# Sinkhorn routing: one 64-column product for the column sums in place of two, and two reciprocals in place of one

## The chip, the core and the metric

The kernel runs on one core of one Trainium2 chip, as one program. The metric is the device time of one execution in microseconds (us). The five engines have a queue of instructions each and run beside one another: TensorE (PE in the profile, with its weight loads as PEld), VectorE (DVE), ScalarE (ACT), GpSimd (POOL) and SyncE (SP, which here only issues transfers). They wait for one another through semaphores. On-chip data lies in SBUF, results of products in the banks of PSUM; both have 128 partitions.

## The reference

Everything is in 32-bit floats. An attention block with polynomial sketches makes x, of 4352 tokens by 128. A router then balances a matrix P of 4352 tokens by 8 experts with eight Sinkhorn iterations, and eight experts' two-layer networks are summed with P as weights:

```python
logits = x @ w_gate                       # N = 4352, E = 8
P = np.exp(logits - logits.max())
for _ in range(8):
    P /= P.sum(1, keepdims=True) + 1e-09  # each token's row
    P /= P.sum(0, keepdims=True) + 1e-09  # each expert's column
    P *= N / E
for e in range(E):
    out += P[:, e:e+1] * (np.maximum(x @ w1[e], 0.0) @ w2[e])
```

The change is in the column sums and their reciprocals, inside that loop of eight.

## The kernel before, in words

The program has three stages that overlap. The attention stage makes x transposed (tile `xT`, 128 features by 4352 tokens). The unweighted stage runs experts 0 and 1 on part of the tokens while routing isn't finished: `first` (L772) multiplies a 128-feature weight tile with up to 416 tokens into a PSUM bank, ScalarE applies relu into `hb` (L774), VectorE forms differences of these results (L787), and `into` (L836) multiplies results and differences with the second weights and accumulates in four banks `s`. When a group of tokens is complete, ScalarE copies the four banks out (L695 to L712) and VectorE adds the copies (L685, L688). The weighted stage (L1158 and after) does the remaining experts after routing, on x that is already multiplied with P.

TensorE is used in the first two stages as two column halves: a product of 128 rows and 64 columns goes either to the lower half (results in partitions 0 to 63) or to the upper half (64 to 127), and the two halves run beside each other. The order of TensorE's queue is the program's, one queue for both halves. An `into` step for one block holds p1 and p6, then p2 and p4, then p3 and p5, then p7. p1, p2 and p3 read plain results and go to the lower half; p4 to p7 read differences, p4, p5 and p6 go to the upper half, and p7 alternates from block to block. Each step of four L772/L836 products stands some steps behind the one that made its inputs (`LAG = 8` steps).

Routing (`routing`, below) is a generator. P lies in SBUF as 128 partitions by 34 by 8. In one iteration VectorE sums the rows (L602), takes reciprocals (L603), scales (L605) and sums each partition's part of the columns into `cs`, 128 by 8 (L608). Then comes a `yield`: the driver calls `fill`, which puts steps of the unweighted stage into the queues. After it, TensorE adds the 128 partitions by a product with a matrix of ones (L612), which leaves every column sum in every partition of the bank; VectorE takes the reciprocals (L615) and scales P for the next iteration (L618). Since the order of VectorE and TensorE is the program's own (`manual_schedule`), VectorE's queue is: L608, the differences and additions that `fill` put in, L615, L618, L602 and so on. After the eighth iteration VectorE transposes P (L622) and SyncE writes it to DRAM (`pT`, L624), from where the weighted stage loads rows of it, repeated over all partitions (`pb`, L1064). GpSimd multiplies x by them (L1071) and makes sums of weights (L984 to L988).

The banks `a` come from a pool of four, in rotation: the banks of L772 and that of the column sums share it.

Of the kernel before, what the change touches and what calls it, by code (L numbers as in the profile page):

```python
# [11 lines left out]
F32 = mybir.dt.float32  # L12
# [40 lines left out]
def kernel(  # L53
# [12 lines left out]
    nc = tc.nc  # L66
    P = nc.NUM_PARTITIONS
# [3 lines left out]
    E = moe_w_gate.shape[1]  # L71
# [14 lines left out]
    sk = ctx.enter_context(tc.tile_pool(name="sk", bufs=2))  # L86
# [10 lines left out]
    def bank():  # L97
        return aps.tile([P, 512], F32, tag="a", name="a")
# [14 lines left out]
    ones = consts.tile([P, P], F32, name="ones")  # L113
    nc.gpsimd.memset(ones, 1.0)
    warm = [aps.tile([P, 512], F32, tag="a", name="a") for _ in range(2)]
    for _ in range(6):
        for r in range(2):
            for c in range(2):
                rows, cols = slice(64 * r, 64 * (r + 1)), slice(64 * c, 64 * (c + 1))
                nc.tensor.matmul(warm[r][cols, 0:256], ones[rows, cols], ones[rows, 0:1].to_broadcast([64, 256]),  # L120
                                 start=True, stop=True, tile_position=(64 * r, 64 * c))
# [373 lines left out]
    def logits(c):  # L495
        lo, hi = chunks[c]
        pg = bank()[:, 0:hi - lo]
        for b in range(B):
            nc.tensor.matmul(pg[32 * b:32 * (b + 1)], wg, xT[:, b * S + lo:b * S + hi], start=True, stop=True,  # L499
                             tile_position=(0, 32 * b))  # L500
        lgs.append((c, pg))
# [3 lines left out]
    def logits_turned():  # L505
        c, pg = lgs.pop(0)
        lo, hi = chunks[c]
        nc.vector.transpose(out=lgp[:, lo // 32:hi // 32, :].rearrange("p a e -> p (a e)"), in_=pg)
# [69 lines left out]
    def routing():  # L578

        yield 5  # L580
        for c in range(len(chunks)):
            logits(c)
            yield 0.6
            logits_turned()
        lg = lgp[:, :, 0:E]
        mx = sk.tile([P, 1], F32, tag="mx", name="mx")
        nc.vector.tensor_reduce(out=mx, in_=lg, axis=AX.XY, op=Alu.max)
        yield 2.2
        pm = bank()[:, 0:P]
        for s in range(2):  # L590
            nc.tensor.matmul(pm[64 * s:64 * (s + 1)], mx.to_broadcast([P, 64]), ident, start=True, stop=True,
                             tile_position=(0, 64 * s))
        nc.vector.reduce_max(mx, pm, axis=AX.X)
        nc.vector.tensor_scalar(mx, mx, -1.0, 64 * math.log(2.0), op0=Alu.mult, op1=Alu.add)
        pw = p2s[0]
        nc.scalar.activation(out=pw[:, :, 0:E], in_=lg, func=Act.Exp, bias=mx[:, 0:1])

        step = 1.5 * 2.0 ** (23 - 149 + 64)
        nc.vector.tensor_scalar(pw[:, :, 0:E], pw[:, :, 0:E], step, step, op0=Alu.add, op1=Alu.subtract)
        for it in range(ITERS):  # L600
            rs = sk.tile([P, SA], F32, tag="rs", name="rs")
            nc.vector.reduce_sum(rs, pw, axis=AX.X)  # L602
            nc.vector.reciprocal(rs, rs)  # L603
            p1 = p1s[it % 2]
            nc.vector.scalar_tensor_tensor(p1[:, 0:SA], rs.unsqueeze(2).to_broadcast([P, SA, E]), UP,  # L605
                                           pw[:, :, 0:E], op0=Alu.mult, op1=Alu.mult)
            cs = sk.tile([P, E], F32, tag="cs", name="cs")
            nc.vector.reduce_sum(cs, p1.rearrange("p g e -> p e g"), axis=AX.X)  # L608
            yield 4.25
            pc = bank()[:, 0:E]  # L610
            for s in range(2):
                nc.tensor.matmul(pc[64 * s:64 * (s + 1)], ones[:, 0:64], cs, start=True, stop=True,  # L612
                                 tile_position=(0, 64 * s))
            cr = sk.tile([P, E], F32, tag="cr", name="cr")
            nc.vector.reciprocal(cr, pc)  # L615
            last = it == ITERS - 1
            pw = lgp if last else p2s[(it + 1) % 2]
            nc.vector.scalar_tensor_tensor(pw[:, :, 0:E], cr.unsqueeze(1).to_broadcast([P, SA, E]),  # L618
                                           float(N) / E * (1.0 if last else UP), p1[:, 0:SA],
                                           op0=Alu.mult, op1=Alu.mult)  # L620

        nc.vector.transpose(out=lgT.rearrange("p a s -> p (a s)"), in_=lgp.rearrange("p a e -> p (a e)"))  # L622
        for b in (1, 0, 2, 3):
            nc.sync.dma_start(out=pT[:, b * S:(b + 1) * S],  # L624
                                                  in_=lgT[32 * b:32 * b + E].rearrange("p a s -> p (a s)"))
# [977 lines left out]
    with tc.manual_schedule(engines={engines.DVE, engines.PE}):  # L1603
# [38 lines left out]
        for i, n in enumerate(routing()):  # L1642
            if i == 0:
                next(made)
            for _ in range(2 if i > 4 else 0):
                fill(n / 2)
                next(made, None)
            if i < 5:
                fill(n)
# [55 lines left out]
```

## Time and profile before

| what | value |
|---|---|
| three runs | 883.72, 882.86, 883.63 us, median 883.63 |
| the profiled execution | 883.02 us, of which the profile's span is 881.2 |
| TensorE products, weight loads | 875.6 us (99%), 572.4 us (65%) |
| VectorE | 724.0 us (82%), 982 instructions |
| ScalarE, GpSimd | 384.6 us (44%), 262.8 us (30%) |
| granted TensorE clock | full over the whole span |
| column-sum products L612 | 16 products, 32 records, from 123.4 to 170.2 us |
| their reciprocals L615 | 8, from 124.5 to 171.0 us |

How to read it. Busy time is the union of an engine's instructions; the rest of the span it was idle. A row of the timeline gives the start, the time taken, the engine, the line, the operation, output and inputs by the program's names, output and input shapes, how many instructions are merged in the row, and in brackets the idle time ahead of it with what ended it. Each product of this kernel appears as two records of TensorE. [...] A row of the waits has the waiting engine, the tile and line, what it waited for, the total in us, how often, and the longest.

### The profile page before, as it was taken

The numbers are of one execution on the slowest core, as the hardware profiler recorded it, in microseconds if no ns is written. First come the engines' busy times: TensorE is split into PE (matmuls) and PEld (weight loads), VectorE is DVE, ScalarE is ACT, GpSimd is POOL, SyncE is SP. The second block draws the span as 40 slices with busy tenths as digits, with TensorE's granted clock in tenths as the row PEclk, the third lists the DMA queues.
The fourth block names the chain that finished last, engine by engine and source line by source line (L and its number), as shares of the span: only waits on it lengthen the run. The fifth ranks groups of instructions, "written<-read, shape, count | busy, mean of one in ns | idle before, by whom it ended". The sixth has DMA issues, their size and how long they took to land.

```text
span 881.2 us, 26159 instructions
## 1 busy us (share of the span) xinstructions
PE 875.6 (99%) x10828; PEld 572.4 (65%) x10828; DVE 724.0 (82%) x982; ACT 384.6 (44%) x792; POOL 262.8 (30%) x254
## 2 busy tenths in 40 slices
PE   9999999999999999999999999999999999999998
PEld 6788656877788655555555555555555566667876
DVE  8699689978888887778887778888788888888896
ACT  3455557644444433333343333334443344444442
POOL 3131125454433313222222222221323323312431
PEclk9999999999999999999999999999999999999999
DMA  8888399886666554444435544434755557567762
GB/s 260 270 273 264 96 233 245 130 260 195 197 195 198 171 160 128 136 144 128 129 94 144 137 125 126 117 115 109 194 152 148 154 139 216 152 152 220 219 194 49
DMA packets 120887, 149.08 MB, mean 169 GB/s; under 512 B 52288, under 2 KB 79808, under 8 KB 120384
## 3 DMA queue, kind: packets, MB, share of 16 engines
q1 hardware_dynamic: 112656, 136.92, 54.4%
q0 software_dynamic: 6720, 10.19, 5.8%
q8 instruction: 86, 1.41, 0.6%
q10 hardware_dynamic: 1392, 0.28, 0.2%
q14 instruction: 33, 0.27, 0.1%
HBM read 104.86 MB, written 25.99 MB: 148 GB/s over the span
## 4 chain that ended last, share of the span: by engine, by line
PE 99%; DMA 0%; DVE 0%; issue 0%; SPq 0%; DVEq 0%
PE pair L1158 39%; PE s L1311 39%; PE a L772 9%; PE s L836 7%; PE a L336 1%; PE a L465 1%; PE a L306 0%; DMA kx<-in_k_dram 0%; PE s L1323 0%; PE s L375 0%; PE a L429 0%; PE s L395 0%; PE a L499 0%; PE a L375 0%; PE a L395 0%; PE a L612 0%
## 5 line engine op out<-in xcount | busy, mean ns | idle before, releaser
L1158 PE MATMUL pair<-xf,w1x 64*64 64x320 f32 (+3 forms) x4496 | 574.1, 466 | 0.1
L1311 PE MATMUL s<-hb,w 64*64 64x480 f32 (+3 forms) x2544 | 363.4, 466 | 0.0
L1158 PEld LDWEIGHTS pair<-xf,w1x 64*64 64x64 f32 x4496 | 251.9, 133 | 116.7 <-issue 63.5
L1174 DVE CUSTOM_DVE_ANT_0 hb<-pair,copies 128x960 f32<-128x960 f32 (+3 forms) x234 | 214.8, 918 | 101.9 <-PE pair L1158 90.0
L1311 PE MATMUL s<-hb,ws 64*64 64x480 f32 (+3 forms) x1888 | 280.7, 468 | 0.0
L1311 PEld LDWEIGHTS s<-hb,w 64*64 64x64 f32 x2544 | 150.2, 133 | 76.3 <-issue 38.6
L1311 PEld LDWEIGHTS s<-hb,ws 64*64 64x64 f32 x1888 | 113.0, 133 | 56.6 <-issue 29.3
L1071 POOL TENSOR_TENSOR xf<-xT,pb 128x960 f32<-128x960 f32 (+3 forms) x40 | 70.3, 1759 | 241.0 <-ACT turn L1364 184.3
L1079 POOL TENSOR_TENSOR xf<-xf 128x960 f32<-128x960 f32 (+3 forms) x39 | 68.1, 1745 | 222.9 <-ACT turn L1364 141.1
L1171 ACT ACTIVATE hb<-pair 128x640 f32<-128x640 f32 (+3 forms) x86 | 66.4, 773 | 150.2 <-PE pair L1158 148.4
L772 PE MATMUL a<-xT,w 128*64 128x416 f32 (+3 forms) x512 | 123.0, 465 | 0.0
L774 ACT ACTIVATE hb<-a 128x416 f32<-128x416 f32 (+3 forms) x128 | 59.5, 468 | 65.7 <-PE a L772 60.5
L1216 DVE TENSOR_TENSOR hb<-hb 128x960 f32<-128x960 f32 (+3 forms) x78 | 74.8, 959 | 7.9 <-PE pair L1158 0.9
L1364 ACT COPY turn<-s 128x1 f32<-128x1 f32 x134 | 20.9, 156 | 137.5 <-PE s L1311 137.5
L1223 DVE TENSOR_TENSOR hb<-hb 128x960 f32<-128x960 f32 (+3 forms) x78 | 72.8, 933 | 7.4
L1219 DVE TENSOR_TENSOR hb<-hb 128x960 f32<-128x960 f32 (+3 forms) x78 | 75.0, 961 | 2.4 <-ACT hb L1171 0.6
L1252 ACT COPY copies<-pair 128x960 f32<-128x960 f32 (+3 forms) x78 | 59.9, 768 | 35.5 <-PE pair L1158 35.4
L1248 ACT COPY copies<-pair 128x960 f32<-128x960 f32 (+3 forms) x78 | 60.1, 770 | 33.0 <-PE pair L1158 33.0
L1243 ACT COPY copies<-pair 128x960 f32<-128x960 f32 (+3 forms) x78 | 59.9, 768 | 33.0 <-PE pair L1158 28.8
L1220 DVE TENSOR_TENSOR hb<-hb 128x960 f32<-128x960 f32 (+3 forms) x78 | 71.9, 922 | 0.0
L836 PE MATMUL s<-hb,ws 128*64 128x416 f32 (+3 forms) x224 | 71.6, 474 | 0.0
L787 DVE TENSOR_TENSOR hb<-hb 128x416 f32<-128x416 f32 (+7 forms) x84 | 56.8, 679 | 13.5 <-ACT hb L774 10.7
(207 smaller groups left out, 663.2 us busy)
## 6 DMA issues: line engine op xcount, KB each, us to landing
w1x<-w1x SPq DMA_DIRECT2D x87, 256.0 KB, 3.7
w<-w2x SPq DMA_DIRECT2D x71, 256.0 KB, 3.0
ws<-w2x SPq DMA_DIRECT2D x35, 256.0 KB, 3.5
pb<-pT SPq DMA_DIRECT2D x14, 480.0 KB, 4.2
xf<-xf SPq DMA_DIRECT2D x28, 240.0 KB, 3.5
w1x<-w1x SPq DMA_DIRECT2D x7, 896.0 KB, 5.9
ws<-w2x SPq DMA_DIRECT2D x36, 128.0 KB, 3.6
pb<-pT SPq DMA_DIRECT2D x13, 320.0 KB, 3.9
```

The costliest lines, as they stand in the source:

```text
L772: nc.tensor.matmul(ph[sl], loaded_w[j][0][:, P * f + H2 * s:P * f + H2 * (s + 1)], xT[:, at + lo:at + hi], start=True, stop=True, tile_pos ...
L836: nc.tensor.matmul(sums[g][i][H2 * s:H2 * (s + 1)], w, x, start=c == 1, stop=c == per, tile_position=(0, H2 * s))
L1071: nc.gpsimd.tensor_tensor(xf[:, 0:2].rearrange("p b n -> p (b n)"), xT[:, lo:lo + 2 * n], weights.pop(i), op=Alu.mult)
L1079: nc.gpsimd.tensor_tensor(xf[:, 4:6], xf[:, 1:4:2], xf[:, 0:2], op=Alu.subtract)
L1158: nc.tensor.matmul(out[H2 * col:H2 * (col + 1), r], w1[rows, PLACE[form], o:o + H2], xf[rows, x], start=start, stop=stop, tile_position=(H ...
L1171: nc.scalar.activation(out=x, in_=y, func=Act.Relu)
L1174: nc.vector._custom_dve(TENSOR_ADD_SAT, out=flat(out, n), in0=x, in1=flat(y, n), s0=math.inf, s1=0.0)
L1216: nc.vector.tensor_tensor(ts[0], h[3], h[0], op=Alu.subtract)
L1219: nc.vector.tensor_tensor(ts[1], h[3], h[1], op=Alu.subtract)
L1220: nc.vector.tensor_tensor(ts[2], h[1], ts[0], op=Alu.subtract)
L1223: nc.vector.tensor_tensor(ts[3], h[2], ts[2], op=Alu.subtract)
L1311: nc.tensor.matmul(out_[H2 * half:H2 * (half + 1)], w[rows], flat(x, n)[rows, r], start=c == 1, stop=True, tile_position=(H2 * rho, H2 * h ...
```

## The change

The two products of ones with `cs`, one to the upper and one to the lower half, become one, to the lower half. The sums then stand in partitions 0 to 63 of the bank alone. VectorE reads these 64 partitions twice, and writes the reciprocals into the lower and then into the upper 64 partitions of `cr`. The order of everything else on all engines stays. Lines after L612 move up by one in the changed program.

```diff
-            pc = bank()[:, 0:E]
+            pc = bank()[0:64, 0:E]
+            nc.tensor.matmul(pc, ones[:, 0:64], cs, start=True, stop=True, tile_position=(0, 0))
+            cr = sk.tile([P, E], F32, tag="cr", name="cr")
             for s in range(2):
-                nc.tensor.matmul(pc[64 * s:64 * (s + 1)], ones[:, 0:64], cs, start=True, stop=True,
-                                 tile_position=(0, 64 * s))
-            cr = sk.tile([P, E], F32, tag="cr", name="cr")
-            nc.vector.reciprocal(cr, pc)
+                nc.vector.reciprocal(cr[64 * s:64 * (s + 1)], pc)
             last = it == ITERS - 1
             pw = lgp if last else p2s[(it + 1) % 2]
             nc.vector.scalar_tensor_tensor(pw[:, :, 0:E], cr.unsqueeze(1).to_broadcast([P, SA, E]),
```

## The prediction

> **What bounds the kernel now.** I read the page first, top to bottom.
>
> ```profile
> span 881.2 us, 26159 instructions
> PE 875.6 (99%) x10828; PEld 572.4 (65%) x10828; DVE 724.0 (82%) x982; ACT 384.6 (44%) x792; POOL 262.8 (30%) x254
> DVE  8699689978888887778887778888788888888896
> PE 99%; DMA 0%; DVE 0%; issue 0%; SPq 0%; DVEq 0%
> ```
>
> TensorE is busy 99% and the chain that ended last is TensorE for 99%. So a change moves the end only if it shortens TensorE's own stream or makes it wait. The slices say where a wait can arise: VectorE is at 9 in the seventh and eighth slice, 132 to 176 us, which is the routing. So next the window of that stage, and TensorE's waits from 120 to 190 us.
>
> ```profile
> 120.00:175.00 55.00, 55.00 (x353) 38.70 (x351) 50.97 (x96) 36.64 (x77) 27.24 (x28) 1.00 1.02 203
> ```
>
> ```profile
> PEld s L836 <- DVE hb L787: 0.8, 3, 0.3
> PEld pair L1158 <- POOL w1x L988: 0.7, 1, 0.7
> ```
>
> The third pair of numbers in the window is VectorE: 50.97 us of 55, so little idle time is left to swallow more work. TensorE still counts as busy throughout, but its weight loads wait three times for VectorE's differences (L787): in this stage VectorE already sets TensorE's pace at single points. That is where the change acts.
>
> **The change part by part.** One of two products goes, and one reciprocal becomes two, in each of 8 iterations.
>
> ```profile
> L612 PE MATMUL a<-cs,ones x32: 172/188/203, 123.4 to 170.2; 128*64 128x8 f32 x32
> ...
> L615 DVE RECIPROCAL cr<-a x8: 192/200/207, 124.5 to 171.0; 128x8 f32<-128x8 f32 x8
> ```
>
> ```profile
> 170.19 0.23 PE L612 MATMUL a<-cs,ones 128*64 128x8 f32 x2
> 170.28 0.89 PE L772 MATMUL a<-xT,w 128*64 128x416 f32 x3
> ```
>
> *TensorE.* A product is two records (32 for 16 products). What one costs its column half is the distance to the next product's start, 170.28 - 170.19 = 0.09 us, far less than the record's 0.19. The two products stand on different halves, each beside the other half's work. Dropping the second relieves the upper half alone, by at most 8 x 0.09 = 0.72 us; the lower half keeps its product. The relief counts only where the upper half isn't waiting for something later anyway.
>
> [...]
>
> *VectorE.* The second reciprocal has 8 columns too. Halving the partitions saves nothing: below, the 64-partition sum takes 0.59 us like the 128-partition one ahead of it. So the first reciprocal stays at 0.20 us, and the price of the edit is the distance from the first's start to the second's.
>
> ```profile
> 124.47 0.20 DVE L615 RECIPROCAL cr<-a 128x8 f32<-128x8 f32 x1
> 124.70 0.45 DVE L618 SCALAR_TENSOR_TENSOR p<-cr,p 128x272 f32<-128x272 f32 x1
> ...
> 135.68 1.22 DVE L787 TENSOR_TENSOR hb<-hb 128x416 f32<-128x416 f32 x2
> 136.82 0.58 DVE L685 TENSOR_TENSOR z<-z,w 128x416 f32<-128x416 f32 x1
> 137.43 0.59 DVE L685 TENSOR_TENSOR kept<-z,f 128x416 f32<-128x416 f32 x1
> 138.04 0.59 DVE L685 TENSOR_TENSOR kept<-z,m 64x416 f32<-64x416 f32 x1
> ```
>
> Three spacings are on show. An independent instruction on the same partitions starts 0.08 us before its predecessor ends (136.82 against 135.68 + 1.22 = 136.90): price 0.20 - 0.08 = 0.12. The sum into the upper 64 partitions (kept<-z,m) doesn't need the one ahead of it, yet starts 0.02 after its end (138.04 against 137.43 + 0.59): price about 0.215, taking half of the rounded 0.02 and more. A dependent one starts 0.03 after (124.70 against 124.67): price 0.235. The second reciprocal is the middle case, independent and writing from partition 64 after one that wrote from 0. I take 0.215; the ends are 0.12 and 0.235. A price below zero is excluded, since an instruction is added and none gets shorter.
>
> [...]
>
> The added reciprocal waits only for the first. Behind it on VectorE's queue stand the iteration's chain (L618, L602, L603, L605, L608) and then the differences L787, for which TensorE waits at L836. The bank is given back one reciprocal later; no wait row of TensorE names L615.
>
> *What swallows the price, and what passes it on.* VectorE's idle times, and the second to fourth iteration:
>
> ```profile
> 130.84 0.58 DVE L688 TENSOR_TENSOR kept<-x,m 64x416 f32<-64x416 f32 x1 [0.74 <-ACT m L702]
> 131.35 0.19 DVE L615 RECIPROCAL cr<-a 128x8 f32<-128x8 f32 x1
> ...
> 138.66 0.21 DVE L615 RECIPROCAL cr<-a 128x8 f32<-128x8 f32 x1
> ...
> 144.45 0.20 DVE L615 RECIPROCAL cr<-a 128x8 f32<-128x8 f32 x1
> ...
> 150.54 0.59 DVE L688 TENSOR_TENSOR z<-x,z 128x416 f32<-128x416 f32 x1 [0.16 <-ACT x L698]
> ...
> 171.74 1.31 DVE L622 STREAM_TRANSPOSE qT<-kT 128x1088 f32<-128x1088 f32 x1
> ...
> 173.87 1.02 DVE L787 TENSOR_TENSOR hb<-hb 128x832 f32<-128x832 f32 x1 [0.39 <-ACT hb L774]
> ```
>
> TensorE's weight loads at the three waits, and after them the starts of the products:
>
> ```profile
> 143.03 0.13 PEld L836 LDWEIGHTS s<-hb,ws 128*64 128x64 f32 x1 [0.30 <-DVE hb L787]
> ...
> 147.76 0.13 PEld L836 LDWEIGHTS s<-hb,ws 128*64 128x64 f32 x1 [0.18 <-DVE hb L787]
> 147.76 0.13 PEld L836 LDWEIGHTS s<-hb,w 128*64 128x64 f32 x1
> ...
> 167.91 0.13 PEld L836 LDWEIGHTS s<-hb,ws 128*64 128x64 f32 x1 [0.27 <-DVE hb L787]
> ```
>
> ```profile
> 143.03 0.56 PE L836 MATMUL s<-hb,ws 128*64 128x416 f32 x1
> ...
> 148.08 0.51 PE L836 MATMUL s<-hb,w 128*64 128x416 f32 x1
> ...
> 168.05 0.49 PE L836 MATMUL s<-hb,ws 128*64 128x384 f32 x1
> ```
>
> ```profile
> 148.98 0.50 ACT L695 COPY z<-s 64x416 f32<-64x416 f32 x1 [0.21 <-PE s L836]
> ```
>
> Step by step, with price d = 0.215:
> Iteration 1 (124.47) is swallowed: VectorE idles 0.74 us before 130.84 for a ScalarE copy that follows TensorE.
> Iterations 2 to 4 (131.35, 138.66, 144.45) lie in back-to-back work, so the difference awaited at 147.76 comes 3d = 0.645 later. At 143.03 the product took 0.56 where others take 0.51: a late weight load costs 0.05 before the product runs. The second load at 147.76 stands behind the waiting one, on the other half; its product began at 148.08, so it had 148.08 - 147.76 - 0.05 = 0.27 to spare. That product completes the group: ScalarE's copies (148.98) follow it, and VectorE's next start (150.54) follows the copies. From there VectorE is 3d - 0.27 = 0.375 late.
> Iterations 5 to 7 add 3d without idle time: at 167.91 the difference is 6d - 0.27 = 1.02 late. Its product at 168.05 had 168.05 - 167.91 - 0.05 = 0.09 to spare, so the upper half is 6d - 0.36 = 0.93 late.
> Iteration 8 saves the upper half its last product, 0.09 us, and its price is swallowed by the 0.39 us of idle time before 173.87.
> Sum: 6 x 0.215 - 0.27 - 0.09 - 0.09 = +0.84 us. After 190 us nothing gives it back: TensorE alone makes up the chain to the end.
>
> The ends: d = 0.12 gives +0.27, d = 0.235 gives +0.96. The profiled execution took 883.02 us (span 881.2 and 1.8 around it), so 883.86 on that basis. The median of the three runs shown is 0.61 above the profiled one, so I forecast 883.63 + 0.84, about 884.5 us. I count as no change what lies within 0.2%, 1.77 us; the three runs alone spread over 0.86 us.
>
> **The rivals.** *Slower: VectorE's lateness reaches the end whole.* The row "pair L1158 <- POOL w1x L988" says that the weighted stage begins when GpSimd lets it, and GpSimd's work hangs on the end of routing:
>
> ```profile
> 173.08 1.35 SPq L624 DMA_DIRECT2D pT<-qT  x4
> 176.81 0.83 SPq L1064 DMA_DIRECT2D pb<-pT  x2
> 177.69 2.54 SPq L960 DMA_DIRECT2D w1x<-in_moe_w_dram  x4
> ```
>
> ```profile
> 184.16 1.15 POOL L985 TENSOR_TENSOR w1x<-w1x 128x256 f32<-128x256 f32 x1 [0.32 <-DMA w1x<-in_moe_w_dram]
> ```
>
> On SyncE's queue the loads of w1x (177.69) stand behind pb, which waits for pT, which waits for the transposition (171.74 + 1.31). If all eight prices arrive there, with the dependent spacing of 0.235, the start moves by 8 x 0.235 = 1.88 us: 885.5. It decides from d = 0.222 on, where 8d passes 1.77, and only if the idle times above swallow nothing. For it: 93% busy VectorE and the row. Against: the 0.74 us before 130.84, and the first products of L1158 read raw forms and weighed x, none of the sums of L984 to L988. Chance 0.31.
>
> *The second reciprocal overlaps the first*, as at 136.82: d = 0.12, +0.27, 883.9. For: both read one bank and neither needs the other. Against: the 138.04 row. Chance 0.10.
>
> *TensorE gains.* VectorE stays ahead, as for most of L836, and the upper half saves 8 x 0.09: -0.72, 882.9. Against: three waits on VectorE and the lower half's unchanged stream. Chance 0.07, and that too lies within 0.2%. A gain of over 1.77 no row can carry: all 16 products together are 1.44. For what would have to come on top I leave 0.06.
>
> **How the numbers follow.** The forecast has 0.46; with the overlap (0.10) and the gain on TensorE (0.07), 0.63 lies within 0.2%; slower 0.31, faster 0.06. Range: from 883.2 (+0.27, less the 0.77 by which one of the three runs lies under the median, rounded up) to 885.9 (the slower rival with some of that spread).
>
> **What would show it.** Each iteration has two reciprocals 0.21 apart (0.12 for the overlap) and one product of two records. L836's waits for L787 grow from 0.8 us to over 2, at the same three places; L622 starts near 173.0, and L1158 near 189.1 instead of 188.3, with the weighted stage unchanged. I am wrong if L1158 moves as far as L622 does, if the waits don't grow, or if time appears after 190 us.

## The result, and the profile after

After takes 884.54 us (median of 22 runs, 883.68 to 886.22), before 883.39 us (median of 22 runs, 882.86 to 884.91). The ratio is 1.0012, with a 95% interval of 1.0007 to 1.0018, so 0.6 to 1.6 us more: slower, but by less than the 0.2% that were counted as no change. Forecast were 884.5 us. The medians lie 1.15 us apart and the profiled executions 0.97 (883.99 against 883.02), where the sum said 0.84.

The page of after: the span, and the busy time of each engine.

```profile
span 882.2 us, 26135 instructions
PE 875.9 (99%) x10812; PEld 567.5 (64%) x10812; DVE 726.1 (82%) x990; ACT 384.3 (44%) x792; POOL 262.6 (30%) x254
```

Eight VectorE instructions came and 16 TensorE records went. VectorE is busy 2.1 us longer, TensorE 0.3 us. The instructions of the two changed lines, with the shortest, median and longest duration in ns, and the first and last start:

```profile
L611 PE MATMUL a<-cs,ones x16: 172/202/223, 123.4 to 170.9; 128*64 128x8 f32 x16
...
L614 DVE RECIPROCAL cr<-a x16: 192/200/202, 124.4 to 172.2; 64x8 f32<-64x8 f32 x16
```

Half the partitions cost the same 0.20 us. VectorE's timeline of after shows the price and where it goes:

```profile
124.41 0.41 DVE L614 RECIPROCAL cr<-a 64x8 f32<-64x8 f32 x2
124.85 0.44 DVE L617 SCALAR_TENSOR_TENSOR p<-cr,p 128x272 f32<-128x272 f32 x1
...
130.78 0.58 DVE L687 TENSOR_TENSOR kept<-x,m 64x416 f32<-64x416 f32 x1 [0.59 <-ACT m L701]
...
172.88 1.31 DVE L621 STREAM_TRANSPOSE qT<-kT 128x1088 f32<-128x1088 f32 x1
...
174.57 1.03 DVE L786 TENSOR_TENSOR hb<-hb 128x832 f32<-128x832 f32 x1
```

From the first reciprocal to the scaling are 0.44 us (before: 124.70 - 124.47 = 0.23), so a second reciprocal costs 0.21. The idle time before 130.8 us fell from 0.74 to 0.59, and that before 173.87 (0.39) is gone. Where the lateness reaches the others:

```profile
PEld s L835 <- DVE hb L786: 2.7, 5, 0.9
...
PEld pair L1157 <- POOL w1x L986: 0.7, 1, 0.7
```

```profile
143.40 0.13 PEld L835 LDWEIGHTS s<-hb,ws 128*64 128x64 f32 x1 [0.72 <-DVE hb L786]
...
148.33 0.13 PEld L835 LDWEIGHTS s<-hb,ws 128*64 128x64 f32 x1 [0.59 <-DVE hb L786]
...
168.84 0.13 PEld L835 LDWEIGHTS s<-hb,ws 128*64 128x64 f32 x1 [0.89 <-DVE hb L786]
```

```profile
149.30 0.50 ACT L694 COPY z<-s 64x416 f32<-64x416 f32 x1 [0.36 <-PE s L835]
...
183.79 0.52 ACT L773 ACTIVATE hb<-a 128x416 f32<-128x416 f32 x1 [0.89 <-PE a L771]
```

```profile
168.85 0.54 PE L835 MATMUL s<-hb,ws 128*64 128x384 f32 x1 [0.17 <-DVE hb L786]
...
189.05 0.50 PE L1157 MATMUL pair<-xf,w1x 64*64 64x320 f32 x4
```

The start of the weighted stage in before:

```profile
188.30 0.77 PE L1158 MATMUL pair<-xf,w1x 64*64 64x320 f32 x8
```

TensorE's waits for VectorE's differences grew from 0.8 to 2.7 us: the same three places hold 2.2 of them. The other two are new, at 186.02 and 188.09 us, with 0.5 us together; what they cost is read off below, under iteration 8. The awaited product at 168.05 starts at 168.85, the weighted stage at 189.05 instead of 188.30.

Executions reach routing at somewhat different times, so from here on a stage is measured from routing's first reciprocal of row sums (L603; 120.75 in before, 120.70 in after) to the first product of the weighted stage: 67.55 us before, 68.35 after. That is 0.80 us of the 0.97; another 0.22 lie after that point, and 0.05 less before it.

### The profile page after: what moved, and what is told of

It reads as the page before. It is cut to its first block, busy times and chain, and to the rows that moved or that the text cites. A ratio compares the mean times of both kernels' runs of the same rounds, so it can differ in the third digit from the quotient of the medians.

```text
span 882.2 us, 26135 instructions
## 1 busy us (share of the span) xinstructions
PE 875.9 (99%) x10812; PEld 567.5 (64%) x10812; DVE 726.1 (82%) x990; ACT 384.3 (44%) x792; POOL 262.6 (30%) x254
## 3 DMA queue, kind: packets, MB, share of 16 engines
q8 instruction: 86, 1.41, 0.7%
## 4 chain that ended last, share of the span: by engine, by line
PE 97%; DVE 2%; DMA 0%; issue 0%; ACT 0%; DVEq 0%
PE pair L1157 39%; PE s L1310 39%; PE a L771 8%; PE s L835 7%; PE a L336 1%; PE a L465 1%; DVE hb L786 1%; PE a L306 0%; PE s L1322 0%; PE s L375 0%; PE a L429 0%; PE s L395 0%; DMA raw<-in_S_dram 0%; PE a L499 0%; DVE rs L602 0%
## 5 line engine op out<-in xcount | busy, mean ns | idle before, releaser
L1157 PE MATMUL pair<-xf,w1x 64*64 64x320 f32 (+3 forms) x4496 | 573.0, 466 | 0.0
L1157 PEld LDWEIGHTS pair<-xf,w1x 64*64 64x64 f32 x4496 | 252.7, 133 | 115.4 <-issue 77.4
```

Source lines behind the costliest of these rows:

```text
L1157: nc.tensor.matmul(out[H2 * col:H2 * (col + 1), r], w1[rows, PLACE[form], o:o + H2], xf[rows, x], start=start, stop=stop, tile_position=(H ...
```

## The experiments

All are before or after with the edit shown. "Stage" is how much later than in before the weighted stage starts, counted from L603, read off the timelines of single profiled executions. The time behind it, where no kernel differs from another, scattered by up to 0.6 us either way, and routing began up to 1.9 us later than in before, so the stage tells more than the median. The medians are of 11 runs (after 22; four_recips, one_128 and pool_sum_after five). Each ratio is to the runs of before made beside that kernel, whose medians were 883.14 to 883.54 us.

| kernel | median us | ratio, 95% interval | stage us |
|---|---|---|---|
| after | 884.54 | 1.0012 [1.0007, 1.0018] | +0.80 |
| dve_only | 885.06 | 1.0018 [1.0010, 1.0027] | +1.77 |
| pe_only | 883.83 | 1.0005 [0.9996, 1.0014] | -0.22 |
| two_products | 884.33 | 1.0013 [1.0004, 1.0021] | +0.92 |
| split_columns | 883.45 | 1.0002 [0.9994, 1.0011] | +0.09 |
| four_recips | 888.28 | 1.0054 [1.0042, 1.0067] | +3.92 |
| outer_four | 884.25 | 1.0008 [0.9999, 1.0018] | +0.55 |
| outer_change | 882.91 | 0.9997 [0.9988, 1.0006] | +0.25 |
| gpsimd_pad | 883.34 | 1.0002 [0.9993, 1.0011] | +0.02 |
| gpsimd_add | 884.14 | 1.0008 [0.9999, 1.0018] | +0.79 |
| one_128 | 888.30 | 1.0053 [1.0039, 1.0066] | +4.38 |
| pool_sum | 885.43 | 1.0019 [1.0010, 1.0028] | +1.76 |
| pool_sum_after | 886.81 | 1.0041 [1.0026, 1.0055] | +2.31 |

### The two parts of the change, each alone

**dve_only**: before, with the reciprocals by halves.

```diff
-            nc.vector.reciprocal(cr, pc)
+            for s in range(2):
+                nc.vector.reciprocal(cr[64 * s:64 * (s + 1)], pc[64 * s:64 * (s + 1)])
```

> Two products as before, but two reciprocals, each half of the partitions for itself: VectorE's part of the change alone. Theory (VectorE's lateness, passed on in six of eight iterations): the two reciprocals start 0.21 us apart, L836's waits for the differences grow from 0.8 to about 2.7 us, and the time is 6 x 0.215 - 0.27 - 0.09 = 0.93 us above before (ratio 1.0011). Rival (the one product on a single half upsets TensorE's two halves): without that product nothing is lost, ratio 1.0000.

Measured 1.0018, stage +1.77, where 0.93 us was expected: VectorE's part alone starts the weighted stage about a microsecond later than the whole change does. **pe_only**: one product into 64 partitions and one reciprocal of these, into two tiles `crs` that are filled with a constant ahead of routing (not shown). It leaves out the reciprocals of the upper 64 partitions, so P is not scaled rightly there.

```diff
-            pc = bank()[:, 0:E]
+            pc = bank()[0:64, 0:E]
-            for s in range(2):
-                nc.tensor.matmul(pc[64 * s:64 * (s + 1)], ones[:, 0:64], cs, start=True, stop=True,
-                                 tile_position=(0, 64 * s))
-            cr = sk.tile([P, E], F32, tag="cr", name="cr")
-            nc.vector.reciprocal(cr, pc)
+            nc.tensor.matmul(pc, ones[:, 0:64], cs, start=True, stop=True, tile_position=(0, 0))
+            cr = crs[it % 2]
+            nc.vector.reciprocal(cr[0:64], pc)
```

> One product into 64 partitions and one reciprocal of these 64; the upper 64 partitions of the reciprocals are a constant that was set at the start, so P is scaled wrongly there: TensorE's part of the change alone. Theory: VectorE does as much as before, the three waits stay near 0.8 us in all, and the upper half's spared products gain little, 0 to 0.3 us, since the upper half waits for VectorE at 143 us and the lower half keeps its product (ratio 0.9997 to 1.0000). Rival (TensorE's stream is what counts): all eight spared products show, -0.72 us, 0.9992. Rival (a single product upsets the halves): slower, near the 1.0012 of the whole change.

Measured 1.0005 with an interval over zero, stage -0.22. The spared products are no gain that the time shows; the two parts don't add up to the change (1.77 - 0.22 is not 0.80). The reason is in VectorE's timeline, here around one reciprocal of dve_only:

```profile
165.78 0.96 DVE L788 TENSOR_TENSOR hb<-hb 128x768 f32<-128x768 f32 x1
166.77 0.42 DVE L616 RECIPROCAL cr<-a 64x8 f32<-64x8 f32 x2
```

The reciprocal starts 0.03 after its predecessor's end (165.78 + 0.96 = 166.74); in before (164.64 against 163.76 + 0.96 = 164.72) and after it starts 0.08 ahead of it. A start behind the predecessor's end happened in seven of the eight iterations, in before and after only in the third, though the product had ended 0.2 to 1.8 us earlier by its records. In dve_only the last read of a bank began at partition 64; in after, both reciprocals read from partition 0. **two_products** keeps both products and reads as the change does:

```diff
-            nc.vector.reciprocal(cr, pc)
+            for s in range(2):
+                nc.vector.reciprocal(cr[64 * s:64 * (s + 1)], pc[0:64])
```

> Before with its two products, but the reciprocals as in the change: both read the lower 64 partitions of the bank, one writes the lower and one the upper 64 partitions of cr. What the upper product leaves in the bank is not read. The question is why the reciprocals by halves behind two products, each half reading its own sums, moved the weighted stage by 1.77 us and the change by only 0.80. Theory (where the bank was read last): in that kernel VectorE's last read of a PSUM bank in an iteration starts at partition 64 and the next one at partition 0, and the first reciprocal starts 0.01 to 0.03 us after its predecessor's end instead of 0.08 before it, in seven of eight iterations. Here all reads start at partition 0, so it starts 0.08 before the end in all iterations but the third, and the time is the change's plus the one product of 0.09 us: weighted stage 0.9 us later than before, ratio 1.0010, about 884.4 us. Rival (TensorE): the spared product is what makes the change cheaper; then this kernel, which keeps both, moves the weighted stage by 1.7 to 1.8 us, ratio 1.0020, about 885.3 us, and the reciprocals start 0.08 before the end all the same.

```profile
164.61 0.96 DVE L788 TENSOR_TENSOR hb<-hb 128x768 f32<-128x768 f32 x1
165.49 0.41 DVE L616 RECIPROCAL cr<-a 64x8 f32<-64x8 f32 x2
```

Measured 1.0013, stage +0.92, and the start is 0.08 ahead of the end again (165.49 against 165.57). So what separates dve_only from the change is mostly not the spared product, which is worth 0.92 - 0.80 = 0.12 us in all (one execution of each), but from which partition the bank is read: six starts 0.09 to 0.11 later make 0.5 to 0.7 of the 0.85 us between dve_only and two_products. The traces put it at 0.59: the product that starts at 182.62 in before starts 1.51 later in dve_only and 0.92 later in two_products. The rest comes in at 186 us, on the way that outer_four shows below.

### How large the price is, and how many of the eight count

**split_columns**: before, with two reciprocals of four columns over all 128 partitions. One instruction more, no other partitions.

```diff
-            nc.vector.reciprocal(cr, pc)
+            for s in range(2):
+                nc.vector.reciprocal(cr[:, 4 * s:4 * (s + 1)], pc[:, 4 * s:4 * (s + 1)])
```

> Two products as before, and two reciprocals that split the 8 columns 4 and 4, both over all 128 partitions. Theory: what holds the second reciprocal is that it writes from another partition than the first; here it does not, so it starts about 0.12 us after the first, and the time is 6 x 0.12 - 0.36 = 0.36 us above before (1.0004). Rival (any second reciprocal waits for the first to end): 0.21 us apart and 0.93 us, 1.0011.

```profile
144.93 0.24 DVE L616 RECIPROCAL cr<-a 128x4 f32<-128x4 f32 x2
145.21 0.45 DVE L619 SCALAR_TENSOR_TENSOR p<-cr,p 128x272 f32<-128x272 f32 x1
```

Measured 1.0002, stage +0.09. The pair overlaps: from the first to the scaling are 0.28 us, 0.05 more than before, where halves of the partitions cost 0.21. The second reciprocal starts 0.08 before the first one's end, where that of after starts 0.01 behind it: this overlap is 0.10 of the 0.16 between the two prices. What after has in its place is another starting partition of the output, and 64 partitions; these alone prevent no overlap, as before's reciprocal at 131.35 starts 0.07 ahead of the end of an addition over 64 partitions (130.84 + 0.58). The rest is the shorter duration: a reciprocal of four columns takes 0.16 us (the median), one of eight 0.20.

**four_recips**: after, each reciprocal twice.

```diff
-            for s in range(2):
+            for s in (0, 1, 0, 1):
```

> The changed kernel with the pair of reciprocals made twice (lower, upper, lower, upper; the second pair writes the same values again): three more than before, each held until the one ahead is done, d = 3 x 0.215 = 0.645 us per iteration. Theory: the first iteration's price still falls into the 0.74 us of idle time before 130.84 and the eighth's does not reach TensorE, so 6 x 0.645 - 0.45 = 3.4 us (ratio 1.0039). Rival (VectorE's lateness reaches the end whole): 8 x 0.645 = 5.2 us (1.0058).

Measured 1.0054, nearer to the rival's number, with the expected 1.0039 outside the interval. The stage says otherwise: +3.92. From the first reciprocal to the scaling are 0.92 us, so the price is 0.69. By the prediction's steps that makes 6 x 0.69 - 0.27 - 0.09 = 3.78 (1.0043, inside the interval); eight prices that arrive whole would make 5.5. Iteration by iteration, the reciprocals start at 0, 0, 0.70, 1.39, 1.83, 2.52, 3.19 and 3.87 us later than in before: nothing from iteration 1, then 0.7 from each, with 0.25 lost between the fourth and the fifth. Some 0.9 us between this stage and the median stay unexplained; the profiled execution reached routing 1.41 us later than that of before, ahead of all that was edited.

**outer_four**: before, with four reciprocals by halves in iterations 1 and 8 only.

```diff
+            for s in (0, 1, 0, 1) if it in (0, ITERS - 1) else ():
+                nc.vector.reciprocal(cr[64 * s:64 * (s + 1)], pc[64 * s:64 * (s + 1)])
+            if it not in (0, ITERS - 1):
...
```

> Before, but with four reciprocals of halves in place of one in the first and the eighth iteration only (d = 0.645 us in each, 1.29 in all); iterations 2 to 7 as before. Theory: both prices are swallowed, the first by the idle 0.74 us before 130.84, the eighth by idle time and by the 2 us that the next differences have to spare, so the time is that of before (1.0000) although the transposition L622 ends later. Rival (VectorE's lateness reaches the end whole, through the end of routing): +1.3 us, 1.0015; if only the eighth counts, +0.65, 1.0007.

Measured 1.0008, stage +0.55, so not swallowed. Iteration 1 is: at the fifth reciprocal nothing of it is left. Iteration 8 isn't, as the rival's second form had it, and its way was new:

```profile
183.74 1.54 POOL L1074 TENSOR_TENSOR xf<-xT,pb 128x640 f32<-128x640 f32 x1 [0.37 <-DMA pb<-pT]
```

```profile
184.12 2.04 DVE L790 TENSOR_TENSOR hb<-hb 128x832 f32<-128x832 f32 x1 [2.77 <-PE s L839]
```

```profile
186.22 0.20 PEld L839 LDWEIGHTS s<-hb,ws 128*64 128x64 f32 x4 [0.77 <-DVE hb L790]
```

VectorE's difference takes 2.04 us beside GpSimd's product of x with P, and TensorE waits 0.77 us for it. The same two rows of before, and of after:

```profile
182.30 1.54 POOL L1071 TENSOR_TENSOR xf<-xT,pb 128x640 f32<-128x640 f32 x1
```

```profile
183.64 1.09 DVE L787 TENSOR_TENSOR hb<-hb 128x832 f32<-128x832 f32 x1 [2.82 <-ACT hb L774]
```

```profile
183.54 1.54 POOL L1070 TENSOR_TENSOR xf<-xT,pb 128x640 f32<-128x640 f32 x1
```

```profile
184.34 1.63 DVE L786 TENSOR_TENSOR hb<-hb 128x832 f32<-128x832 f32 x1 [2.79 <-ACT hb L773]
```

In all three the difference ends 0.88 or 0.89 us after GpSimd's product does (184.73 after 183.84, 185.97 after 185.08, 186.16 after 185.28). A later transposition makes P's rows, and so GpSimd's product, later, and VectorE's difference ends only 0.88 or 0.89 us behind that product.

### The new way, by itself

**gpsimd_pad**: before, with a fill of zeros on GpSimd ahead of its second product. Routing is untouched.

```diff
+        if i == 1:
+            nc.gpsimd.memset(xf[:, 4:8], 0.0)
         nc.gpsimd.tensor_tensor(xf[:, 0:2].rearrange("p b n -> p (b n)"), xT[:, lo:lo + 2 * n], weights.pop(i),
```

> Before, with one more instruction on GpSimd: a fill with zeros of a part of xf that is overwritten later, ahead of the second product of x with P, so that this product runs about 1.1 us later and lies beside the first of the three differences that VectorE makes at 183.6 us. Routing is not touched and VectorE has the same instructions. Theory (VectorE's two-input addition stands still while GpSimd's product runs): that difference takes 1.9 to 2.2 us instead of 1.09 and ends about 0.9 us after GpSimd's product; TensorE waits at the second weights for it, by 0.4 to 0.8 us at 185 to 187 us, and the weighted stage starts 0.3 to 0.5 us later: ratio 1.0004, about 883.9 us. Rival (the addition grew in the other kernels because VectorE itself was late): the difference stays at 1.0 to 1.1 us, TensorE doesn't wait, the weighted stage starts at the same time, ratio 1.0000.

```profile
178.56 1.16 POOL L1072 MEMSET xf<- 128x1280 f32 x1 [7.38 <-PE a L772]
...
184.53 1.55 POOL L1073 TENSOR_TENSOR xf<-xT,pb 128x640 f32<-128x640 f32 x1 [0.35 <-DMA pb<-pT]
```

```profile
185.56 1.40 DVE L787 TENSOR_TENSOR hb<-hb 128x832 f32<-128x832 f32 x1 [2.80 <-ACT hb L774]
```

The edit failed: the fill went into GpSimd's wait for P's rows, and the product ended only 0.32 us later, counted from L603 (this execution reached it 1.92 us later). The difference grew by just that, 0.31. TensorE did not wait. **gpsimd_add** puts an addition there that needs the first product:

```diff
+        if i == 1:
+            nc.gpsimd.tensor_tensor(xf[:, 4], sources[0][:, 0], sources[0][:, 1], op=Alu.add)
```

> Before, with one more addition on GpSimd that reads the first product of x with P (320 columns, into a part of xf that is overwritten later) and so stands between the two products: the second runs some 0.9 us later, not the 0.3 that the fill with zeros gave. Routing is not touched. Theory (VectorE's two-input addition stands still while GpSimd's product runs, and TensorE has about 0.49 us to spare behind it, the value that the kernels with halves give: later by 0.54 lost nothing, by 0.76 lost 0.27, by 0.90 lost 0.41): the difference at 183.6 us takes 1.9 to 2.0 us instead of 1.09, TensorE waits for it by 0.3 to 0.8 us in all at 185 to 188 us, and the weighted stage starts about 0.4 us later: ratio 1.0005. Rival (VectorE's own lateness made it grow): the difference stays below 1.4 us, the weighted stage starts at the same time, ratio 1.0000.

```profile
183.93 1.55 POOL L1073 TENSOR_TENSOR xf<-xT,pb 128x640 f32<-128x640 f32 x1
```

```profile
184.01 2.35 DVE L787 TENSOR_TENSOR hb<-hb 128x832 f32<-128x832 f32 x1 [2.81 <-ACT hb L774]
```

```profile
186.42 0.20 PEld L836 LDWEIGHTS s<-hb,ws 128*64 128x64 f32 x4 [0.98 <-DVE hb L787]
```

The difference took 2.35 us, TensorE waited 0.98, and the stage started 0.79 later, with routing as before. All three are more than expected, since the product came 1.25 us later, not 0.9. So the mechanism is shown apart from any change in routing. Where this difference decides, the stage is its end less a constant: 1.04 later gave 0.55 (outer_four), 1.25 gave 0.79, 2.26 gave 1.77 (dve_only). TensorE has 0.46 to 0.49 us to spare there.

**outer_change**: the change itself, in iterations 1 and 8 alone.

```diff
+            outer = it in (0, ITERS - 1)
+            pc = bank()[0:64 if outer else P, 0:E]
+            for s in range(1 if outer else 2):
...
+            if outer:
+                for s in range(2):
+                    nc.vector.reciprocal(cr[64 * s:64 * (s + 1)], pc)
```

> The change in iterations 1 and 8 alone: there one product into 64 partitions and two reciprocals, in the six others as before. Theory (the place decides, not the number of reciprocals): iteration 1's price of 0.215 goes into VectorE's 0.74 us of idle time before 130.8 us; iteration 8's shows in the transposition, 0.2 us later, but VectorE's idle time of 0.39 us before 173.9 takes it, and by way of P's rows GpSimd's product ends 0.2 to 0.5 us later, which stays within the 0.49 us that TensorE has to spare behind the difference at 183.6 us. Weighted stage -0.1 to +0.1 us against before, ratio 1.0000. Rival (each iteration's price reaches the end): two prices of 0.215, weighted stage 0.4 us later, ratio 1.0005; if each iteration bore an eighth of the change's 0.80, 0.2 us later.

```profile
171.98 1.31 DVE L627 STREAM_TRANSPOSE qT<-kT 128x1088 f32<-128x1088 f32 x1
...
173.91 1.02 DVE L792 TENSOR_TENSOR hb<-hb 128x832 f32<-128x832 f32 x1 [0.19 <-ACT hb L779]
```

Counted from L603 (0.04 later here), the transposition is 0.20 late and the difference at 173.9 not at all: VectorE's idle time takes iteration 8's price, as forecast. Yet the stage came out at +0.25, over the 0.1 expected, because GpSimd's second product ended 0.71 later; more than half of that is not the 0.20 but P's rows landing later, which they also did in pe_only (0.23, with an earlier transposition). The time is 0.9997 of before's, with an interval over zero: these two iterations cost nothing that can be measured, the change in all eight does (1.0012), so the six between them bear it.

### Other forms

**one_128**: one product over all 128 columns in place of two halves, one reciprocal.

```diff
-            for s in range(2):
-                nc.tensor.matmul(pc[64 * s:64 * (s + 1)], ones[:, 0:64], cs, start=True, stop=True,
-                                 tile_position=(0, 64 * s))
+            nc.tensor.matmul(pc, ones, cs, start=True, stop=True)
```

> One product of ones into all 128 partitions over the whole array width, and one reciprocal as before. [...] With 0.2 for two changes, up to 0.2 for halves that stand apart by a part of a product, and 0.09 less, +0.2 to +0.35 us per iteration, 1.6 to 2.8 us (1.0018 to 1.0032). Rival (fewer products are cheaper whatever their width): 0 to -0.7 us.

```profile
145.11 0.30 PEld L611 LDWEIGHTS a<-cs,ones 128*128 128x128 f32 x2 [0.65 <-ACT hb L772]
```

```profile
145.54 0.21 DVE L613 RECIPROCAL cr<-a 128x8 f32<-128x8 f32 x1 [0.56 <-PE a L611]
```

Measured 1.0053, stage +4.38, more than expected: 0.55 us an iteration on average. The weight load of the wide product stood idle 0.65 us, and the next products of either half start at 145.43; VectorE then waited 0.56 for the sums. The 0.2 for two changes (of the product's width, there and back) in the expected sum is shown by no run apart; the rows show the 0.65 ahead of the load and 0.32 from the load to the next products (145.11 to 145.43). What held the load wasn't tried apart.

**pool_sum** gives one of VectorE's additions to GpSimd for five token groups, to make up for the price; **pool_sum_after** is the same on after.

```diff
...
-            add_now(y1[lower], own["p1"][lower], m[lower])
+            add_now(y1[lower], own["p1"][lower], m[lower], nc.gpsimd if 1 < g < 7 else nc.vector)
```

> Before, with one addition of each group of tokens (the first of the two into the kept sums, L688, second of the pair) on GpSimd in place of VectorE. Theory: VectorE no longer idles for ScalarE's copy at 130.84 and 151.33 and has 0.6 us less to do per group, so the three waits for the differences vanish, and the upper half gets back the 0.4 us it lost at 143: ratio 0.9995. Rival (GpSimd's addition stands behind its transfers and holds up ScalarE's next copies, or slows VectorE): slower than before.

> The changed kernel with that same addition on GpSimd. Theory: the second reciprocal costs only where VectorE has no time to spare; with 0.6 us and the idle time given back per group, its price disappears, so this is equal to the kernel above (0.9995 of before, 1.3 us under the changed kernel). Rival (the price is on a path of its own, through the single product or the end of routing): 0.8 to 1 us slower than the kernel above.

```profile
131.71 1.20 DVE L618 SCALAR_TENSOR_TENSOR p<-cr,p 128x272 f32<-128x272 f32 x1
...
163.75 2.16 DVE L685 TENSOR_TENSOR kept<-z,m 64x416 f32<-64x416 f32 x1
```

```profile
164.03 1.42 POOL L688 TENSOR_TENSOR kept<-x,m 64x416 f32<-64x416 f32 x1
```

Both were slower (1.0019, 1.0041), where 0.9995 was expected. In pool_sum the second reciprocal (131.35 in before) came 0.53 us earlier, but the scaling behind it took 1.20 us, in place of 0.44, beside an addition of GpSimd's, at 163.75 an addition that takes 0.59 alone took 2.16 beside GpSimd's 1.42, and the seventh reciprocal came 1.5 us later than in before. At 163.75 alone VectorE lost 1.57 us, more than the 0.59 that one moved addition spares it. pool_sum_after's stage is 0.55 later than pool_sum's. Its five runs (885.69 to 888.44) don't agree well enough to say more.

## Why the prediction was right, point by point

**The price.** Taken was 0.215 (bounds 0.12 and 0.235); measured 0.21. That the starting partition of the output holds the second reciprocal is shown by split_columns, where the output starts at the same partition and the two overlap by 0.08. Its price of 0.05 is lower than the bound taken from the additions, since reciprocals of four columns are also shorter.

**TensorE.** One sparing of 0.09 was counted, not 0.72. two_products puts all eight spared products together at 0.12, pe_only at 0.22 with VectorE as before, and in pe_only's median nothing of it shows. The rival that TensorE gains has fallen.

**What passes the price on.** Each step has its row; all are counted from L603, which is 0.05 earlier in after.

| step | forecast us | measured us |
|---|---|---|
| iteration 1 swallowed by VectorE's idle time | 0 left | 0 (131.29 against 131.35) |
| iterations 2 to 4: weight load at 147.76 | 0.645 | 148.33: 0.62 |
| to spare at 148.08, then ScalarE's copy at 148.98 | 0.375 | 149.30: 0.37 |
| iterations 5 to 7: weight load at 167.91 | 1.02 | 168.84: 0.98 |
| to spare at 168.05: its product | 0.93 | 168.85: 0.85 |
| transposition L622, "near 173.0" | 1.26 | 172.88: 1.19 |
| weighted stage, "near 189.1" | 0.84 | 189.05: 0.80 |

**Iteration 8** was forecast to vanish in the idle time before 173.87. It did there (outer_change). What the step lacked is the second way out of the transposition, over P's rows and GpSimd's product to VectorE's difference at 184 us. It cost after next to nothing, but only just: the difference ends 1.29 late, of which 0.46 to 0.49 are spare, so 0.80 to 0.83 would arrive by this way, and TensorE's products were as late already by the forecast chain. The rows of before, of one half, then the same products of after and the two new waits:

```profile
182.62 0.51 PE L836 MATMUL s<-hb,ws 128*64 128x416 f32 x1
...
187.16 0.51 PE L836 MATMUL s<-hb,ws 128*64 128x416 f32 x1
```

```profile
183.35 0.51 PE L835 MATMUL s<-hb,ws 128*64 128x416 f32 x1
...
187.89 0.51 PE L835 MATMUL s<-hb,ws 128*64 128x416 f32 x1
```

```profile
186.02 0.61 PEld L835 LDWEIGHTS s<-hb,ws 128*64 128x64 f32 x5 [0.26 <-DVE hb L786]
...
188.09 0.28 PEld L835 LDWEIGHTS s<-hb,w 128*64 128x64 f32 x2 [0.24 <-DVE hb L786]
```

This half is 0.78 late ahead of the first new wait and 0.78 late behind it; the other half is 0.75 late at both places (182.83 against 183.53, 187.02 against 187.72). So in after the lateness came by the forecast chain, and the second way added at most some 0.03, the last step from 0.78 to the stage. In dve_only it added 0.26, in outer_four 0.41. That the missing term was next to nothing in the change itself is luck: nothing in the prediction kept it small.

**The signs.** The waits grew as forecast at the same three places, but there are five of them, not three. 0.22 us appeared after the weighted stage's start, where the prediction had nothing; that is within the 0.6 by which this stretch scattered between kernels that are alike there, so this sign decides nothing.

**The time.** The 884.5 were 883.63 + 0.84. That 884.54 came is partly luck of the base: the median of the first three runs lies 0.24 above the 883.39 of all 22, and the medians moved by 1.15, which is 0.31 more than the sum. The step that the sum describes, the start of the weighted stage, was met to 0.04.

**The slower rival** (lateness reaches the end whole, by GpSimd's sums of w1x) fell as stated:

```profile
188.71 0.72 POOL L987 TENSOR_TENSOR w1x<-w1x 128x256 f32<-128x256 f32 x1
```

The last of these sums ends at 189.43, after the weighted stage began at 189.05, and the transposition moved by 1.19 where the stage moved by 0.80. The row "pair L1157 <- POOL w1x" with the same 0.7 us in both kernels is not a wait on these sums. But the rival had the right road, transposition to rows to GpSimd, with another vehicle: it ends at VectorE, and it decides only where its lateness, less the 0.46 to 0.49 us to spare, is more than that of the forecast chain.

## What to carry to other kernels

Splitting a short VectorE instruction by partitions cost a whole further instruction here (0.21 us), since the other starting partition kept it from overlapping; splitting it by columns cost a quarter of that (0.05). What an added instruction costs the kernel is found iteration by iteration, from what each engine has to spare at the next point where it is awaited, and all ways out of the last iteration have to be followed, those through another engine's instructions too (GpSimd's product, 0.55 us in outer_four). An addition moved from VectorE to GpSimd wasn't free for VectorE: in pool_sum an addition of VectorE's that takes 0.59 us alone took 2.16 beside the moved one.

## What the runs showed of the hardware that was not expected

Where GpSimd's product of 640 columns began first, the end of VectorE's difference of 832 columns near 184 us hung on it: in before, after and six further kernels (dve_only, split_columns, outer_four, gpsimd_pad, gpsimd_add, outer_change) the difference ended 0.88 to 0.89 us after that product, though it had started between 0.20 us (before) and 1.47 us (gpsimd_add) ahead of the product's end. It took 1.09 to 2.35 us there; one at 173.87 in before, beside no instruction of GpSimd's, took 1.02. Where a VectorE addition began first, the product took longer than its 1.54 us: 2.12 in before, from 198.70 on, beside an addition from 198.07 to 199.42. Beside GpSimd's shorter sums of 256 columns both engines took longer: in before VectorE's differences of 416 columns at 184.76 and 185.80 took 1.00 us each, against 0.59 at 175.52, and the sums at 184.16 and 185.28 took 1.15 and 1.07, against 0.73 at 187.46. In pool_sum VectorE's addition at 163.75 started 0.28 us ahead of GpSimd's at 164.03 and still took 2.16; why stays open.

A reciprocal that read a bank from partition 0, when the last read of a bank had begun at partition 64, started 0.09 to 0.11 us later (dve_only against two_products), with 9 to 12 other VectorE instructions between the two reads. In outer_four, where only iterations 1 and 8 read from partition 64, the reciprocal of iteration 2 is the one that starts later (0.03 behind its predecessor's end, in before 0.07 ahead of it).
